# Fewer and larger first loads, two feed-forward tiles by rows of x, and v cast in pairs of heads, in a fused linear-attention and GEGLU kernel

## The chip, the cores and the metric

One core of a Trainium2 chip runs the whole program. The metric is the device time of one execution in microseconds (us), taken over several executions. "Ratio" is the estimate from the fast runs of one kernel and of the kernel before in the same rounds, with a 95% interval; below 1 is faster. "So many us faster" below is the difference of the plain means of all these runs. Only kernels of one set of rounds are compared closely.

## The reference, cut to what matters

```python
# q, k, v: (8 batches, 8 heads, 576 rows, 64), float32
q_s = softmax(q, over the 64 columns of a head)
k_s = softmax(k, over the 576 rows)
kv  = einsum('bhsd,bhse->bhde', k_s, v)           # 64 x 64 per head
x   = einsum('bhsd,bhde->bhse', q_s, kv)          # -> (4608, 512)
out = (gelu(x @ w_gate) * (x @ w_val)) @ w_out    # 512 -> 1536 -> 512
```

## The kernel before

The kernel runs batch by batch on TensorE (PE): feed-forward tiles `psg` and `psv` (12 pairs per batch, eight 128x512 matmuls a pair), then the output product `psy`. The attention of the next batches is threaded between them ("ride"). The parts that the change and the argument touch:

```python
def load(src, nm, b, h0, h1, n0):          # two transfers of 64 partitions each, on SyncE's queue
    ...
    for t in range(2):
        nc.sync.dma_start(out=tiles[key][t:P:2, h0:h1, n0 * D:NC * D], in_=...)

def cast_v(b, h0, h1, eng="pool"):         # f32 -> f16, one instruction
    copy_on(eng, v16_b[b % 2][:, :, h0:h1, 0:D].rearrange("p n h d -> p h n d"),
            tiles[("v", b)][:, h0:h1, :].rearrange("p h (n d) -> p h n d", d=D))

def norm_mul(b, hp, eng="dve"):            # q softmax: e *= 1/sum, both inputs in SBUF
    ...
def warm_pe(n):                            # n matmuls whose result nobody reads
    ...
def ffn_first(xt, after):                  # several tiles at once: rows 0 and 1 of x, then 2, then 3
    ...

# start: twelve first transfers, by halves of the heads
for src, nm, n0 in ((q, "q", 1), (k, "k", 0), (v, "v", 0)):
    for h0 in (0, 4):
        load(src, nm, 0, h0, h0 + 4, n0)
...
# batches 2 to 7: v of all heads cast on GpSimd, one batch ahead
at(b, FI, NFI - 1, L(exp, "q", b + 2), L(exp, "k", b + 2), L(cast_v, b + 2, 0, H))
...
# only batch 1 uses ffn_first
if b == 1:
    hts = ffn_first(xt, first1)
```

Engine names in the profile: DVE is VectorE, ACT is ScalarE, POOL is GpSimd, SP is SyncE.

The softmax here doesn't subtract the row's maximum and nothing guards it: scores larger than these inputs give would overflow.

## Time and profile before

| | before |
|---|---|
| median of the first three runs | 333.1 us (332.79 to 333.62) |
| profiled span | 330.8 us |
| PE busy | 317.1 us, 96% |
| VectorE, ScalarE, GpSimd busy | 56%, 44%, 12% |
| PE's first matmul of the third feed-forward tile of batch 0 | 22.14 us |
| PE's first matmul of batch 1's fourth tile | 59.57 us |
| from there to the end | 271.22 us |

The lines of the profile before stand in the prediction.

### The profile page before, as it was taken

The page shows a single profiled execution, that of the slowest core. Times are in us where ns is not written, and L with a number is a line of the kernel's source. Part 1 is how long each engine was busy: PE and PEld are TensorE (multiplying, and loading weights), DVE is VectorE, ACT ScalarE, POOL GpSimd, SP SyncE. Part 2 cuts the span into 40 slices and gives each one's busy share as a digit, 9 for nine tenths or more (in the row PEclk, how much of TensorE's full clock was granted, in tenths as well). Part 3 has the DMA queues.
Part 4 walks back from the last instruction along what each step waited for, and adds up shares of the span by engine and source line. Part 5 has one row for each costly group of instructions (what it writes and reads, how often), then busy time and mean ns, then how long its engine had stood idle before and what let it go on. Part 6 is the DMA issues. An engine that isn't in the chain of part 4 may idle for free.

```text
span 330.8 us, 4451 instructions
## 1 busy us (share of the span) xinstructions
PE 317.1 (96%) x1700; PEld 151.9 (46%) x1700; DVE 183.9 (56%) x327; ACT 146.7 (44%) x196; POOL 41.0 (12%) x40
## 2 busy tenths in 40 slices
PE   7699999997999999999999999999999999999994
PEld 2334444444455544544454445444544444444441
DVE  4743375499579736962599238832983234333331
ACT  3553564896353582349134932474243033103300
POOL 1377462211000200020002000200000000000000
PEclk9799999999999999999999999999999999999999
DMA  6999999970177015900491029301100110040002
GB/s 189 356 383 391 402 393 391 395 263 0 63 247 294 2 53 164 387 2 0 164 389 53 2 106 355 144 0 65 63 0 2 63 63 2 0 110 17 4 32 95
DMA packets 38453, 50.49 MB, mean 153 GB/s; under 512 B 2208, under 2 KB 34208, under 8 KB 38432
## 3 DMA queue, kind: packets, MB, share of 16 engines
q1 hardware_dynamic: 38288, 50.08, 42.7%
q8 instruction: 13, 0.21, 0.3%
q10 hardware_dynamic: 144, 0.13, 0.1%
q14 instruction: 8, 0.07, 0.1%
HBM read 40.76 MB, written 9.44 MB: 152 GB/s over the span
## 4 chain that ended last, share of the span: by engine, by line
PE 77%; DMA 9%; DVE 5%; ACT 3%; SPq 2%; issue 2%; POOL 1%; DVEq 0%; ACTq 0%; POOLq 0%
PE psy L308 26%; PE psg L264 23%; PE psv L264 22%; DMA wvst<-in_moe_w_val_dram 4%; DMA qt<-in_q_dram 3%; PE pskv L190 2%; DVE eq L163 2%; DMA kt<-in_k_dram 2%; PE psx L242 2%; PE pst L215 2%; DVE rq L156 1%; SPq L103 1%; ACT eq L143 1%; DVE ht L271 1%; ACT L143 1%
## 5 line engine op out<-in xcount | busy, mean ns | idle before, releaser
L269 ACT ACTIVATE gl<-psg 128x512 f32<-128x512 f32 x108 | 64.0, 598 | 140.3 <-PE psg L264 130.3
L271 DVE SCALAR_TENSOR_TENSOR ht<-psv,gl 128x512 f16<-128x512 f32 x108 | 73.8, 688 | 65.3 <-PE psv L264 61.0
L264 PE MATMUL psg<-xt,wg_sb 128*128 128x512 f16 x384 | 100.1, 379 | 0.7 <-ACT xt L121 0.5
L264 PE MATMUL psv<-xt,wv_sb 128*128 128x512 f16 x384 | 99.5, 379 | 0.1
L308 PE MATMUL psy<-wo_sb,ht 128*128 128x512 f16 x432 | 95.8, 379 | 0.0
L264 PEld LDWEIGHTS <-wv_sb 128*128 128x128 f16 x432 | 42.2, 98 | 51.9 <-issue 1.4
L308 PEld LDWEIGHTS <-ht 128*128 128x128 f16 x432 | 41.7, 98 | 48.4 <-DVE ht L271 0.2
L264 PEld LDWEIGHTS <-wg_sb 128*128 128x128 f16 x432 | 40.9, 98 | 45.0 <-issue 1.8
L342 DVE TENSOR_SCALAR yo<-psy 128x512 f32<-128x512 f32 x31 | 21.2, 687 | 48.6 <-PE psy L308 48.6
L119 POOL CAST v<-vt 128x2560 f16<-128x2560 f32 (+1 forms) x7 | 14.9, 2123 | 148.2 <-DMA vt<-in_v_dram 140.6
L156 DVE TENSOR_REDUCE rq<-eq 128x10 f32<-128x640 f16 (+1 forms) x32 | 25.4, 793 | 9.5 <-ACT eq L143 9.3
L163 DVE TENSOR_TENSOR eq<-eq,rrq 128x640 f16<-128x640 f16 (+1 forms) x27 | 26.0, 963 | 0.9
L121 ACT CAST xt<-psx 128x512 f16<-128x512 f32 x27 | 15.1, 587 | 16.8 <-PE psx L242 16.8
L143 ACT ACTIVATE eq<-qt 128x2560 f16<-128x2560 f32 (+1 forms) x9 | 18.5, 2051 | 4.7 <-DMA qt<-in_q_dram 4.6
L143 ACT ACTIVATE ek<-kt 128x2048 f16<-128x2048 f32 (+1 forms) x10 | 15.6, 1560 | 3.7 <-DMA kt<-in_k_dram 3.7
L215 PE MATMUL pst<-ident,eq 128*128 128x128 f16 x128 | 11.1, 226 | 4.9 <-DVE eq L163 2.8
L215 PEld LDWEIGHTS <-eq 128*128 128x128 f16 x128 | 8.7, 100 | 9.9 <-POOL eq L163 2.7
L190 PE MATMUL pskv<-v,ek 128*128 128x130 f16 x160 | 12.0, 220 | 1.2 <-DVE v L123 1.1
L190 PEld LDWEIGHTS <-ek 128*128 128x128 f16 x160 | 10.4, 97 | 4.7 <-issue 1.5
L264 PE MATMUL psg<-xtr,wg_sb 128*128 128x512 f16 x48 | 12.3, 379 | 0.0
L264 PE MATMUL psv<-xtr,wv_sb 128*128 128x512 f16 x48 | 12.3, 379 | 0.0
L242 PE MATMUL psx<-eqt,kv_sb 128*128 128x512 f16 x32 | 10.8, 380 | 1.1 <-DVE kv_sb L198 0.9
(52 smaller groups left out, 131.8 us busy)
## 6 DMA issues: line engine op xcount, KB each, us to landing
qt<-in_q_dram SPq DMA_DIRECT2D x14, 640.0 KB, 6.8
kt<-in_k_dram SPq DMA_DIRECT2D x12, 640.0 KB, 8.2
vt<-in_v_dram SPq DMA_DIRECT2D x12, 640.0 KB, 9.7
out_dram<-yo SPq DMA_DIRECT2D x14, 512.0 KB, 3.1
wost<-in_moe_w_out_dram SPq DMA_DIRECT2D x6, 512.0 KB, 8.8
kt<-in_k_dram SPq DMA_DIRECT2D x8, 320.0 KB, 6.8
vt<-in_v_dram SPq DMA_DIRECT2D x8, 320.0 KB, 6.6
wgst<-in_moe_w_gate_dram SPq DMA_DIRECT2D x5, 512.0 KB, 7.4
```

Of the source, the lines that this page charges most:

```text
L121: nc.scalar.copy(out=dst, in_=src)
L143: nc.scalar.activation(out=dst[:, c0:c1, h0 * D:h1 * D].rearrange("p n (h d) -> p h n d", d=D), in_=tiles[(nm, b)][:, h0:h1, c0 * D:c1 * D ...
L156: nc.vector.reduce_sum(rq, e, axis=mybir.AxisListType.X)
L163: (nc.gpsimd if eng == "pool" else nc.vector).tensor_tensor(out=e, in0=e, in1=rrq.unsqueeze(-1).to_broadcast((P, n, 2, D)), op=ALU.mult)
L190: nc.tensor.matmul(pskv[:, j, :], ek_b[b % 2][:, n, hp * P:(hp + 1) * P], v16_b[b % 2][:, n, 2 * hp:2 * hp + 2, 0:VW], start=(n == 0), sto ...
L215: nc.tensor.transpose(pst[:, j, n * P:(n + 1) * P], eq_b[b % 2][:, n + 1, hp * P:(hp + 1) * P], ident)
L242: nc.tensor.matmul(psx, st[(b, "kv", hp)].rearrange("p h e -> p (h e)"), st[(b, "eqt")][:, hp, 0:MAIN], start=True, stop=True)
L264: nc.tensor.matmul(ps, w[:, ci, fi * P:(fi + 1) * P], xt[:, ci, :], start=(ci == 0), stop=(ci == HP - 1))
L269: nc.scalar.activation(out=gl, in_=psg, func=ACTF.Gelu)
L271: nc.vector.scalar_tensor_tensor(out=ht, in0=psv, scalar=_H_SCALE, in1=gl, op0=ALU.mult, op1=ALU.mult)
L308: nc.tensor.matmul(psy, hts[fi][:, ns * P:(ns + 1) * P], wo_sb[:, fi, :], start=(fi == 0), stop=(fi == NFI - 1))
L342: nc.vector.tensor_scalar(out=yo, in0=psy, scalar1=1.0 / _H_SCALE, scalar2=None, op0=ALU.mult)
```

## The change

Its intent: fewer transfers ahead of the weights, no wait of PE for the last two rows of x before the first feed-forward tile, and no long GpSimd instruction beside VectorE. The order of the start and the warm-up matmuls follow.

```diff
     def cast_v(b, h0, h1, eng="pool"):
+        if eng == "pool" and h1 - h0 > 2:
+            for h in range(h0, h1, 2):
+                cast_v(b, h, h + 2)
+            return
...
     for src, nm, n0 in ((q, "q", 1), (k, "k", 0), (v, "v", 0)):
-        for h0 in (0, 4):
-            load(src, nm, 0, h0, h0 + 4, n0)
+        load(src, nm, 0, 0, H, n0)
...
-    warm_pe(14)
+    warm_pe(16)
...
     unit_t(0, 0, "dve")
-    warm_pe(4)
+    warm_pe(6)
     cast_v(0, 0, 4, "dve")
+    cast_v(0, 4, 6, "act")
     unit_t(0, 1, "dve")
+    cast_v(0, 6, 8, "pool")
     unit_kv(0, 0)
-    warm_pe(2)
-    cast_v(0, 4, 6, "act")
-    cast_v(0, 6, 8, "dve")
+    unit_kv(0, 1)
     unit_x(0, 0, "act", True)
     unit_x(0, 1, "act", True)
-    unit_kv(0, 1)
...
-    unit_x(0, 2, "act", True)
+    unit_x(0, 2, "dve", True)
     unit_x(0, 3, "dve", True)
...
+    first = {0: [[], []], 1: first1}
...
-        if b == 1:
-            hts = ffn_first(xt, first1)
-            fi0 = 3
-            ride(b, FI, 2)
+        if b in first:
+            hts = ffn_first(xt, first[b])
+            fi0 = len(hts)
+            ride(b, FI, fi0 - 1)
```

## The prediction

> **What bounds the kernel now.** I read the page's slices first, then the chain of work that ended last, then the timeline of the places where TensorE (PE) stands idle, and last the transfer rates of the first microseconds.
>
> ```profile
> PE   7699999997999999999999999999999999999994
> PEclk9799999999999999999999999999999999999999
> DMA  6999999970177015900491029301100110040002
> ```
>
> PE is full in nearly all 40 slices of 8.27 us. Of the 330.8 us, the page gives PE 317.1 busy, so at most 13.7 us are to be had in all, and nearly all of it lies in the first two slices and in slice 10. The DMA line is full in slices 1 to 7 only: transfers can bind the first 60 us and nothing later. A change that touches the start and the v casts can therefore move the total by a few microseconds at most.
>
> The chain of waits, in order of time, says what sets the step from batch 0 to batch 1 (columns: start us, us, what):
>
> ```profile
> 29.25 10.23 DMA qt<-in_q_dram
> ...
> 40.84 2.35 ACT eq L143
> ...
> 46.33 1.27 POOL eq L163
> 47.60 0.05 issue
> 47.65 0.40 PE pst L215 x4
> ```
>
> The load of batch 1's q lands at 39.48, and exp, sums and norms follow without slack until PE transposes it at 47.65. In the timeline PE had come to that unit at 47.17 (its first four transposes), so transfer chain and PE arrive there within about 0.26 us of each other. A faster start of PE alone is lost at 47.65, unless the transfer stream is earlier too.
>
> After that PE has only two marked gaps, both in the timeline (start us, us, engine, line, operation):
>
> ```profile
> 73.58 2.32 POOL L119 CAST v<-vt 128x2560 f16<-128x2560 f32 x1 [10.53 <-DMA vt<-in_v_dram]
> 73.60 2.98 DVE L163 TENSOR_TENSOR eq<-eq,rrq 128x640 f16<-128x640 f16 x1
> ...
> 76.64 0.40 PE L215 MATMUL pst<-ident,eq 128*128 128x128 f16 x4 [1.67 <-DVE eq L163]
> ...
> 175.81 2.33 POOL L119 CAST v<-vt 128x2560 f16<-128x2560 f32 x1 [30.99 <-DMA vt<-in_v_dram]
> ...
> 176.15 2.67 DVE L163 TENSOR_TENSOR eq<-eq,rrq 128x640 f16<-128x640 f16 x1
> ...
> 178.87 0.40 PE L215 MATMUL pst<-ident,eq 128*128 128x128 f16 x4 [0.42 <-DVE eq L163]
> ```
>
> The reader should see that the norm multiplication, whose median over the line is 825 ns, took 2.98 and 2.67 us exactly where GpSimd's 2.3 us cast of v began just before it, and ended about 0.7 to 0.8 us after that cast ended; and that PE then waited for it.
>
> The start of batch 0 and its transfers (windows view: stretch, then busy us of PE, PEld, DVE, ACT, POOL, granted clock, DMA share, GB/s):
>
> ```profile
> 15.08 0.73 ACT L121 CAST v<-vt 128x640 f16<-128x640 f32 x1 [1.89 <-DMA vt<-in_v_dram]
> ...
> 15.88 0.88 DVE L123 CAST v<-vt 128x640 f16<-128x640 f32 x1
> ...
> 18.39 1.32 PE L264 MATMUL psg<-xt,wg_sb 128*128 128x512 f16 x4
> ```
> ```profile
> 4.00:6.00 2.00, 2.00 (x6) 0.65 (x5) 0.09 (x1) 1.06 (x1) 0.00 (x0) 1.00 1.01 287
> 6.00:8.00 2.00, 1.34 (x8) 0.49 (x6) 1.93 (x4) 0.11 (x1) 0.00 (x0) 1.00 0.86 230
> ...
> 12.00:14.00 2.00, 0.84 (x7) 0.35 (x4) 0.62 (x2) 1.20 (x2) 0.65 (x1) 0.68 1.07 389
> ```
>
> The second half of v lands at 15.08, and the feed-forward starts at 18.39. The second tile's first matmul is at 20.41; eight matmuls at the 0.216 us spacing seen later give an effective start of 20.41 - 1.73 = 18.68. Transfers run at 230 to 290 GB/s early, against 389 later, although the engines' busy share is near 1.
>
> **What the Trainium skill says.** "SBUF — State Buffer", section "Who interferes with whom", says a VectorE instruction with two SBUF inputs contends with a GpSimd instruction that reads SBUF, and that the loser blocks for the winner's whole instruction. The trace agrees: 2.98 and 2.67 us instead of 0.825. "DMA: Bandwidth & Descriptors", section "Issuing engines are not separate DMA queues", says that parallel issue saves only sequencer time; here the twelve first loads cost 0.62 to 0.89 us of SyncE each, and the first weight load is issued at 9.36, but the queue is never visibly empty, so I expect little from halving the issues. "TensorE: Matmul & The Clock Gate", section "What's actually happening", says that the clock falls after an idle window and needs a busy one to return, in free-running windows; the trace grants 0.50 in 10 to 12 us and full clock from about 13.3.
>
> **Part 1, the casts in pairs.** It removes six 128x2560 casts of 2326 ns median and adds 24 of 128x640. The one cast of that form in the trace took 716 ns, so one batch's v costs 4 x 0.72 = 2.9 us of GpSimd instead of 2.3; GpSimd is 12% busy, and the result is needed a batch later, so this costs nothing. A norm that meets a cast now waits for one piece, at most 0.72 us, if VectorE gets the port between pieces. At 73.60: piece one ends at 74.30, the multiplication at 75.13, and PE transposes at about 75.17 instead of 76.64: 1.47 us. At 176.15: piece one ends at 176.53, the multiplication at 177.36, before PE needs it at 178.28 (four transposes at 0.055 us after 178.06): 178.87 - 178.28 = 0.59 us. The sum is 2.06 us, on the path since PE is saturated from there to the end. A third collision, at 109.44 (1.26 us instead of 0.69), cost PE nothing. I allow a tenth of this for shifted phases and new small collisions: **1.8 us**.
>
> **Part 2, the six loads.** Each carries twice the bytes at, I take it, the same 0.62 to 0.65 us of issue (batch 1's full q loads, deep in the queue, show a minimum of 0.60). SyncE then reaches the weights near 4.7 us instead of 9.36. But the bytes before v is complete are the same: 1.05 MB of q and 1.18 MB each of k and v, 3.41 MB. The early slowness is mostly slow packets (single packets of 0.2 to 1.3 us, against 46 to 55 ns usually, until about 11.5 us), which I see no reason to go away; idle engines are worth some 0.2 of 2 us at 6 to 8, an estimate from the share of 0.86 against 1.07, so about 0.4 us. So v should be complete at 14.7, plus or minus 0.4. The first halves are lost: q, landed by halves at 4.82 and 7.89, now lands whole at 7 to 8, and v's first half no longer comes at 13.40.
>
> From q at 7.5: exp 1.06 to 8.6; VectorE then has four sums (0.68 + 0.20 each) and two multiplications (0.69), 4.9 us, so until 13.5, then the 0.64 us copy, until 14.1. That fits before v. From v at 14.7: VectorE casts half of v (0.83), GpSimd a quarter at the same moment, and these two contend: the 0.88 us of the cast at 15.88, half the size of the 0.83 us one at 13.40, shows that already. So both are done about 1.6 us later, or VectorE's at 0.85 if it wins. Key-value products follow: 20 matmuls, 1.1 us at full clock, 2.2 at half; then 0.8 us for reciprocal and first scaling, 0.4 for the x product, 0.6 for its copy, partly side by side. Effective start: 14.7 + 0.85 + 1.1 + 0.9 + 0.4 = 17.95 in the good case, 18.7 if GpSimd wins, about 19 if the half clock lasts. Against 18.68 that is a gain of 0.7, 0, or a loss of 0.3.
>
> **Part 3, two tiles by rows.** PE does eight matmuls on rows 0 and 1 of x first, 1.73 us of work that covers the two 0.69 us copies of rows 2 and 3, now both on VectorE. This removes the 0.3 us between 18.39 and 18.68 and makes up for the serial copies. It needs the second tile's weights about 0.9 us earlier; their casts end at 17.90 and 18.69 before, needed at about 18.8 and 19.2: just enough.
>
> What the start can pay is limited at 47.65: transfers earlier by 0.4 plus the 0.26 us of slack, and no more than PE's own gain. Good case 0.6, middle 0.2, bad -0.3: **0.3 us**.
>
> Sum: 333.1 - 1.8 - 0.3 = **331.0 us**.
>
> **Rivals.** (A) The large transfers fill the queues earlier and the stream gains 1 to 1.5 us; then PE and the chain at 47.65 both gain it: about 329.8. For it: the low early rate. Against: SyncE is ahead of the data all the time. (B) The start gets slower, since whole-head loads hold up exp and norms, the clock stays low or GpSimd blocks VectorE's v cast: PE comes to 47.65 a microsecond late: 332. For it: q's first half was at work 3 us sooner. (C) VectorE does not get the port between the pieces and waits for all four, 2.9 us instead of 2.3: then part 1 loses some 0.6 us at each of the two gaps, about 334. Against it: the skill's lock is per instruction, and VectorE is already waiting when a piece ends.
>
> **Range and chances.** The middle is 331.0. A and the good case give the low end, 329.5; B with half of part 1 the high end, 332.9. A fall of over 2% needs 326.4 us, about half of all the PE idle time in the span, and no rival reaches it; a rise over 2% needs 339.8, which not even C reaches.
>
> **What would show it.** Right: 24 casts of about 0.72 us from batch 2 on; no multiplication of line 163's norm above about 1.6 us; no PE gap over 0.5 us at batch 2's last transposes near 75 us nor in the middle batches; batch 1's q landing within 0.5 us of 39.5; feed-forward start between 17.8 and 19. Wrong: q of batch 1 landing a microsecond or more away (A), PE reaching batch 1's transposes late (B), or multiplications of 3 us among the pieces (C).

## The result, and the profile after

The changed kernel took 329.15 us median (329.01 to 329.48, 4 runs) against 332.95 us of before (4 runs): ratio 0.9887, interval 0.9866 to 0.9907. That is below the range of the prediction. In two more sets of rounds the same kernel gave 329.61 us (ratio 0.9928) and 329.3 us (ratio 0.9904). The three gains are 3.77, 2.49 and 3.23 us, mean 3.2; the prediction had 2.1.

The page of the changed kernel, its slices (8.2 us each now; tenths of busy time):

```profile
PE   7699999999999999999999999999999999999994
PEclk9599999999999999999999999999999999999999
DMA  7999999960196016900590039202100110040002
```

The 7 in the tenth slice of PE is gone. The granted clock in the second slice is lower than before (5 instead of 7), and yet the time fell.

The timeline of the changed kernel at the place of the large gap, and at the second one (start us, us, engine, line, operation):

```profile
73.18 0.82 DVE L167 TENSOR_TENSOR eq<-eq,rrq 128x640 f16<-128x640 f16 x1
73.22 3.36 POOL L119 CAST v<-vt 128x640 f16<-128x640 f32 x4 [10.70 <-PE psg L268]
...
74.15 0.61 PE L219 MATMUL pst<-ident,eq 128*128 128x128 f16 x8
...
173.18 3.31 POOL L119 CAST v<-vt 128x640 f16<-128x640 f32 x4 [30.23 <-PE psg L268]
...
173.88 1.36 DVE L167 TENSOR_TENSOR eq<-eq,rrq 128x640 f16<-128x640 f16 x1
...
175.79 0.61 PE L219 MATMUL pst<-ident,eq 128*128 128x128 f16 x8
```

The four pieces need 3.3 us where the one cast needed 2.3. At 173.88 the norm waited for the rest of one piece only, 1.36 - 0.82 = 0.54 us, and PE goes through its eight transposes with no gap marked. At 73.18, however, VectorE was simply first, by 0.04 us; one profile cannot say whether the pieces saved anything there. That needed the experiments.

The chain of waits of the changed kernel at the step from batch 0 to batch 1:

```profile
39.33 7.77 PE psy L312 x36
47.10 0.52 PE pst L219 x8
47.61 1.29 PE psy L312 x6
```

Here PE is bound by itself: no transfer, exp or norm stands between 39.33 and 47.61, where before the load of q1 did.

The start of the changed kernel, and its transfers in the windows view (columns as in the prediction):

```profile
14.03 0.83 DVE L123 CAST v<-vt 128x1280 f16<-128x1280 f32 x1 [0.80 <-DMA vt<-in_v_dram]
14.05 1.38 POOL L119 CAST v<-vt 128x640 f16<-128x640 f32 x1 [0.19 <-DMA vt<-in_v_dram]
...
15.17 1.94 PE L194 MATMUL pskv<-v,ek 128*128 128x130 f16 x20
...
18.32 0.72 PE L268 MATMUL psg<-xt,wg_sb 128*128 128x512 f16 x2
```
```profile
4.00:6.00 2.00, 2.00 (x6) 0.65 (x5) 0.00 (x0) 0.00 (x0) 0.00 (x0) 1.00 1.10 372
6.00:8.00 2.00, 1.38 (x6) 0.45 (x4) 0.38 (x1) 1.47 (x2) 0.00 (x0) 1.00 1.01 344
...
12.00:14.00 2.00, 2.00 (x6) 0.72 (x5) 1.20 (x3) 1.54 (x3) 1.04 (x1) 0.50 1.10 369
```

v lands whole at 14.0, the cast of GpSimd lasts 1.38 us since VectorE's came first, and the key-value products run at half clock. The transfers run at 344 to 372 GB/s where they had 230 to 287. The third tile begins at 21.90, against 22.14 before. So this pair of profiles shows a start 0.24 us better at the third tile and 0.42 us at batch 1's fourth tile (59.15 against 59.57), and 268.55 us from there to the end instead of 271.22. That is 0.42 + 2.67 = 3.1 us, the difference of the two spans.

### The profile page after: what moved, and what is told of

It reads as the page before. It is cut to its first block, busy times and chain, and to the rows that moved or that the text cites. A ratio compares the mean times of both kernels' runs of the same rounds, so it can differ in the third digit from the quotient of the medians.

```text
span 327.7 us, 4481 instructions
## 1 busy us (share of the span) xinstructions
PE 317.5 (97%) x1702; PEld 153.1 (47%) x1702; DVE 180.5 (55%) x327; ACT 146.0 (45%) x195; POOL 46.4 (14%) x59
## 4 chain that ended last, share of the span: by engine, by line
PE 89%; DMA 5%; ACT 2%; DVE 2%; issue 1%; SPq 1%; POOL 0%; POOLq 0%; ACTq 0%
PE psy L312 28%; PE psv L268 26%; PE psg L268 26%; DMA kt<-in_k_dram 3%; PE pskv L194 3%; PE pst L219 2%; PE psx L246 2%; DMA qt<-in_q_dram 1%; PE pswarm L260 1%; SPq L103 1%; ACT xt L121 1%; DVE kv_sb L202 0%; PE pstr L231 0%; DVE rq L160 0%; ACT L143 0%
## 5 line engine op out<-in xcount | busy, mean ns | idle before, releaser
L119 POOL CAST v<-vt 128x640 f16<-128x640 f32 x26 | 20.6, 830 | 141.5 <-PE psx L246 64.3
L167 DVE TENSOR_TENSOR eq<-eq,rrq 128x640 f16<-128x640 f16 (+1 forms) x27 | 23.1, 856 | 0.9
L123 DVE COPY eqt<-pst 128x1024 f16<-128x1024 f16 x16 | 10.9, 679 | 0.6 <-PE pst L219 0.6
```

What stands on the lines that cost most here:

```text
L119: nc.gpsimd.tensor_copy(out=dst, in_=src)
L167: (nc.gpsimd if eng == "pool" else nc.vector).tensor_tensor(out=e, in0=e, in1=rrq.unsqueeze(-1).to_broadcast((P, n, 2, D)), op=ALU.mult)
```

## The experiments

Theories. **C**: the whole casts hold VectorE up by chance, differently in each run, and are worth more than the one profile showed. **S**: the extra gain is in the start. **R**: the pieces had no part in it, VectorE won a race by 0.04 us. **I** came after the first set of rounds: the collision of batch 1 is tied to the landing of v, so that in the kernel before it swallows whatever the start gains, and the parts are worth more together than apart.

### The kernel before once more

No edit.

> The kernel before, unchanged, as a control for the runs and a second profile. Theory C (the GpSimd casts of v as one instruction block VectorE's norm by chance, differently from run to run, and are worth more on average than the one profile showed): ratio 1.000, single runs spread over 1 us or more (332.4 to 333.6 so far), and in this second profile the norms that exceed 1.5 us are at other places or of other lengths than at 73.60 and 176.15. Theory S (the extra gain is in the start, the casts are worth the 2.1 us of the first profile): the same two long norms of 2.98 and 2.67 us within 0.2 us, and spread within 0.5 us.

Ratio 0.9995 (0.9976 to 1.0014), runs from 331.67 to 333.12, median 332.53; the profiled span is 330.8 us again. Timeline:

```profile
73.59 2.32 POOL L119 CAST v<-vt 128x2560 f16<-128x2560 f32 x1 [10.49 <-DMA vt<-in_v_dram]
74.22 2.37 DVE L163 TENSOR_TENSOR eq<-eq,rrq 128x640 f16<-128x640 f16 x1
...
76.65 0.40 PE L215 MATMUL pst<-ident,eq 128*128 128x128 f16 x4 [1.07 <-DVE eq L163]
```

The start of this run was worse: the third tile began at 22.93 instead of 22.14. VectorE came to its norm 0.62 us later than in the first profile (74.22 against 73.60). But GpSimd began its cast at the same moment, 73.59 against 73.58, the norm could end only after the cast, and PE's transposes came at 76.65 against 76.64. Between these two profiles the late start was free, so the early one was lost. Theory C was half met: the runs spread by 1.45 us, but the two long norms are at the same places, one of another length.

### Casts in pairs alone

```diff
     def cast_v(b, h0, h1, eng="pool"):
+        if eng == "pool" and h1 - h0 > 2:
+            for h in range(h0, h1, 2):
+                cast_v(b, h, h + 2)
+            return
```

Three sets of rounds, each beside other kernels:

> Before, with the casts in pairs of heads alone. Theory C: 2.6 to 3.3 us faster than before, spread of single runs at most 0.5 us, no norm above 1.6 us, no marked gap of TensorE after 60 us. Theory S: 2.0 us faster or less. Rival R (VectorE won a race by 0.04 us in the profile after, and the pieces had no part in it): under 1 us faster, with some norm still at 2 us or more.

> Casts in pairs alone, again, so that the start's worth with the casts in pairs is read on one chip. Theory I: 1.8 to 2.6 us faster than before, spread over 1 us or more from the start, whose clock windows fall differently in each run. Rival: equal to the changed kernel within 0.3 us.

> Casts in pairs alone, beside the changed kernel. 1.8 to 2.2 us faster than before, as in the two sets before, with a spread of over 1 us of single runs.

Medians 330.44, 330.61 and 330.85 us; ratios 0.9937, 0.9945 and 0.9953; 1.96, 1.90 and 1.53 us faster than before, mean 1.8. The longest norm from batch 2 on was 0.91, 1.35 and 1.11 us, and no gap of PE is marked after 60 us. The first expectation of theory C, 2.6 to 3.3 us, was too high; S had said 2.0 us or less, which fits. The third set fell short of its 1.8 to 2.2 us. R is out: without any of the start's changes no norm reaches 1.5 us.

The spread stayed (329.78 to 331.34 in the first set), and the profiles put it in the start: the third tile began at 23.88, 22.90 and 23.83 us. In the third of these profiles the windows view shows why; the column after POOL is the granted clock:

```profile
14.00:18.00 4.00, 3.47 (x21) 2.31 (x22) 2.16 (x6) 1.64 (x3) 1.93 (x3) 0.50 1.13 355
18.00:20.00 2.00, 1.35 (x8) 0.65 (x6) 0.78 (x3) 0.31 (x2) 1.11 (x3) 0.50 1.02 357
20.00:24.00 4.00, 4.00 (x18) 1.75 (x17) 1.38 (x2) 3.01 (x5) 2.69 (x3) 0.93 1.09 385
```

PE had half its clock until 20.5 us in that run, into the feed-forward.

### The start alone, and the loads alone

The changed kernel with `cast_v` as before (one instruction), and the kernel before with the six loads.

> The changed kernel with v cast in one instruction of all heads again, so loads, rows and order alone. Theory C: 0.4 to 1.0 us faster than before (batch 1's transposes came 0.4 to 0.5 us earlier in the profile after), with single runs spread as widely as before's. Theory S: 1.5 to 1.9 us faster. Rival R: 2 us or more, since then the start moved VectorE ahead of GpSimd.

> Before with six loads of all heads in place of twelve, order and rows as before. If the six loads alone make the transfer stream earlier: 3.41 MB moved by about 12.4 us instead of 13.5, batch 1's q landing near 39.0 instead of 39.5, and time 0 to 0.5 us faster, limited by TensorE's own arrival. If the stream's gain in the profile after was luck of that run: 3.41 MB at 13.2 us or later, and the time up to 0.5 us slower, since the halves are lost and the second half of v is cast on VectorE after the first.

The start alone: 332.68 us, ratio 0.9998 (0.9975 to 1.0021). The loads alone: 332.5 us, ratio 0.9994. Neither moves the time. S is out in its plain form, and C's 0.4 to 1.0 us for the start alone was missed as well. Timeline of the start alone:

```profile
73.55 2.33 POOL L119 CAST v<-vt 128x2560 f16<-128x2560 f32 x1 [10.43 <-DMA vt<-in_v_dram]
74.10 2.45 DVE L163 TENSOR_TENSOR eq<-eq,rrq 128x640 f16<-128x640 f16 x1
...
76.61 0.40 PE L215 MATMUL pst<-ident,eq 128*128 128x128 f16 x4 [1.15 <-DVE eq L163]
```

76.61 against 76.64 and 76.65, after a third tile at 22.33. The cast begins within 0.04 us of the same moment in these three profiles, and PE goes on only when the norm behind it is done. Two things spoil the picture. In this profile PE had already lost 0.49 us at batch 1's transposes, where VectorE's norm at 44.32 took 1.31 us beside a GpSimd cast of w_out. And with the loads alone the cast came earlier:

```profile
72.96 2.32 POOL L119 CAST v<-vt 128x2560 f16<-128x2560 f32 x1 [10.46 <-DMA vt<-in_v_dram]
74.40 1.55 DVE L163 TENSOR_TENSOR eq<-eq,rrq 128x640 f16<-128x640 f16 x1
...
76.01 0.40 PE L215 MATMUL pst<-ident,eq 128*128 128x128 f16 x4 [0.25 <-DVE eq L163]
```

There PE passed this place 0.6 us sooner, and lost it again to a norm of 2.67 us at 106.5. So the moment is not fixed.

The loads do move the transfers. Adding up the packets of the queue, 3.41 MB, as many bytes as the first q, k and v have, were moved by 12.07 to 12.51 us in all seven profiles with six loads, and by 12.98 to 13.60 us in all eleven with twelve: about 1 us sooner. The time does not follow.

### The changed kernel again, and with twelve loads

> The changed kernel as it is, beside the next three on one chip. Theory I (the collision at batch 1's last norm is tied to the landing of v, so in the kernel before it swallows whatever the start gains, and the parts are worth more together than apart): 3.3 to 4.0 us faster than before, single runs within 0.6 us of each other, and 1.0 to 1.8 us faster than the casts alone. Rival (parts simply add: 2.1 for the casts, 0 for the start, and the first rounds were lucky): about 2.1 us faster, like the casts alone.

> The changed kernel a third time, beside the casts in pairs alone, so that the start's worth is read a second time on one chip. Expected from the second set: 2.2 to 3.2 us faster than before and 0.4 to 1.0 us faster than the casts alone. If the first rounds (3.8 us) were the true size: 3.5 us or more. If the start is worth nothing: equal to the casts alone within 0.2 us.

> The changed kernel with the first batch in twelve transfers by halves again. If the six loads give the start its gain (transfer stream a microsecond earlier): at least 0.5 us slower than the changed kernel, 3.41 MB moved only by 13.2 us, batch 1's transposes waiting for the norm. If the order, the rows and the warm-up give it: within 0.2 us of the changed kernel or faster, since q's first half is back at 4.8.

```diff
-        load(src, nm, 0, 0, H, n0)
+        for h0 in (0, 4):
+            load(src, nm, 0, h0, h0 + 4, n0)
```

The changed kernel was 2.49 and 3.23 us faster than before; beside it the casts alone 1.90 and 1.53. So on top of the casts the start is worth 0.59 us in one set and 1.70 us in the other, about 1.1 us, while alone it was worth nothing. Theory I had forecast 3.3 to 4.0 us, 1.0 to 1.8 us over the casts and runs within 0.6 us for the second set, and missed all three (the runs spread by 1.7 us); the third set came out above its forecasts (3.2 and 1.0 us). That the parts do not add is likely but not settled: the interval of the start alone reaches from 0.7 us slower to 0.8 us faster, and the 0.59 us lie in it. The changed kernel with twelve loads took 329.70 us, ratio 0.9926, against 329.61 and 0.9928 on the same chip: the six loads are worth nothing that these runs resolve. Whole heads bring v in one piece at 14.0, while halves bring its first half at 13.1 and its second at 14.8, and the first half's cast and products then lie under the second half's transfer.

### The two tiles by rows, with the casts

The casts in pairs, and `ffn_first` for batch 0; loads, order and warm-up as before.

```diff
+    first = {0: [[], []], 1: first1}
...
-        if b == 1:
+        if b in first:
```

> Casts in pairs and the two first tiles by rows of x, with loads, order and warm-up as before. If the rows pay by themselves: x rows 2 and 3 come about 0.6 to 0.9 us after row 1, which the eight matmuls of rows 0 and 1 cover, so 0.3 to 0.6 us faster than the casts alone. If the start is lost to the clock and to the casts of v: within 0.2 us of the casts alone.

330.36 us, ratio 0.9933, 2.26 us faster than before, and 0.73 us faster than the casts alone in the same rounds (intervals 0.9914 to 0.9953 and 0.993 to 0.9977, so they overlap). The rows seem to pay, a little more than expected; the size is not settled.

### One long instruction, or the total time of GpSimd?

Both do every cast of v from batch 2 on twice in a row: once as a whole in the kernel before, once in pairs.

```diff
-        copy_on(eng, v16_b[b % 2]..., tiles[("v", b)]...)
+        for _ in range(2 if b >= 2 else 1):
+            copy_on(eng, v16_b[b % 2]..., tiles[("v", b)]...)
```

> The kernel before with the cast of v from batch 2 on done twice in a row, each time as one instruction of all heads (the same result). If VectorE waits for one GpSimd instruction at a time, as long as that instruction lasts: norms of 2 to 3 us, now at more places since GpSimd is at it for 4.6 us per batch, none over 3.3 us, and 0.5 to 3 us slower than before. If what counts is GpSimd's total time at the port: single norms of 4 to 5 us and 3 to 6 us slower.

> Before with the casts in pairs, each pair cast twice, so GpSimd is busy 5.7 us per batch in eight pieces, more than twice the time of the kernel before. If the length of one instruction counts: no norm above 1.7 us, no marked gap of TensorE after 60 us, and the time of the casts in pairs done once, about 2.0 us faster than before, within 0.5 us. If the total time at the port counts: slower than before.

Whole: 332.91 us, ratio 1.0013 (0.9983 to 1.0043), not the 0.5 us slower or more that was expected. Pairs: 331.56 us, ratio 0.9969 (0.9941 to 0.9996). Timeline of the whole casts, then of the pairs:

```profile
73.83 5.19 POOL L119 CAST v<-vt 128x2560 f16<-128x2560 f32 x2 [8.17 <-DMA vt<-in_v_dram]
74.43 2.40 DVE L164 TENSOR_TENSOR eq<-eq,rrq 128x640 f16<-128x640 f16 x1
```
```profile
107.42 6.79 POOL L119 CAST v<-vt 128x640 f16<-128x640 f32 x8 [27.11 <-DMA vt<-in_v_dram]
107.50 1.31 DVE L168 TENSOR_TENSOR eq<-eq,rrq 128x640 f16<-128x640 f16 x1
```

With 5.19 us of casts in two instructions the norm waits for the rest of the first and then runs. With 6.79 us in eight it waits for one. What a norm waits for is the length of one instruction, not GpSimd's total time. From batch 1's fourth tile to the end the doubled pairs took 268.42 us, just like all other kernels with pairs, and the doubled whole casts 270.53. The total time of the doubled pairs missed its expectation (0.9 us faster instead of 2.0 within 0.5): in its profile the start was the worst of all, the third tile at 24.50. With four runs and a start that varies this much I take the tail, not the total, as the answer; that the doubling itself costs part of the missing 1.1 us is not excluded.

### Keeping PE busy before the feed-forward

Three kernels have more warm-up matmuls and nothing else changed: the casts alone (26, 12, 3 in place of 14, 4, 2), the changed kernel (34, 8 in place of 16, 6), and the changed kernel with twelve loads (26, 12, 3, 3).

> Casts in pairs, loads and order as before, but 26, 12 and 3 warm-up matmuls in place of 14, 4 and 2, so that TensorE does not stand idle before the first feed-forward. If the clock's fall before the first feed-forward is what the start of the kernel before loses at random (third tile at 22.1, 22.9, 23.9 and 22.9 us in four profiles of that start): no half clock after 7 us, third tile at 21.8 to 22.2, 0.5 to 1.0 us faster than the casts in pairs alone, that is 2.5 to 3.1 us faster than before and equal to the changed kernel, with six loads and rows worth nothing by themselves. If rows and order are what counts: within 0.2 us of the casts in pairs alone, 2.0 faster than before.

> The changed kernel with more warm-up matmuls (34 and 8 in place of 16 and 6), so that TensorE is busy until its first transposes. If the half clock from 9.7 to 16.5 us costs the start: no half-clock window between 7 and 20 us, key-value products at 0.06 us each instead of 0.11, feed-forward start near 17.4 instead of 18.3, and 0.3 to 0.8 us faster than the changed kernel, the rest held by batch 1's q (exp at 39.1 at best follows its landing). If the start is bound by v's transfer and the casts: within 0.2 us of the changed kernel.

> The changed kernel with loads by halves and with warm-up matmuls between all stages of the start (26, 12, 3, 3). A version meant to beat both: no half clock after 7 us, key-value products and x products at full clock, third tile at 21.0 to 21.5 us, and 0.5 to 1.0 us faster than the changed kernel, 3.0 to 3.5 us faster than before. If the start is bound by transfers and casts rather than by the clock: equal to the changed kernel within 0.3 us.

In all three profiles the clock record shows no half clock from 7.2 us at the latest to the last matmul. The casts with warm-up took 330.14 us, ratio 0.9929, 2.27 us faster than before (expected 2.5 to 3.1), with runs from 329.71 to 330.38: a spread of 0.7 us where the casts alone had 1.6 to 1.8. The changed kernel with warm-up took 329.14 us, ratio 0.9907, 0.67 us faster than the changed kernel in the same rounds, as expected, though the intervals overlap; its feed-forward began at 18.07, not near 17.4, and its runs still spread by 1.4 us. At full clock the third tile began at 22.41 with the old start and at 21.65 with the new one, so the clock is not all that divides the two starts. With twelve loads it took 330.02 us, ratio 0.9929, a miss: its third tile came at 21.26, earlier than in any kernel so far, and then

```profile
46.88 2.48 POOL L167 TENSOR_TENSOR eq<-eq,rrq 128x640 f16<-128x640 f16 x2 [1.94 <-DVE rrq L162]
...
48.19 0.40 PE L219 MATMUL pst<-ident,eq 128*128 128x128 f16 x4 [1.10 <-POOL eq L167]
```

PE stood 1.10 us at batch 1's transposes, since the chain behind q1 was late: q1 landed at 40.02, against 39.00 in the profile with six loads and the longer warm-up. This is the cap that the prediction named at 47.65, and it exists. Whether six loads pay here, with a fast start, is not shown: in the other profile of the new order with twelve loads q1 landed at 39.00 too.

### A version meant to beat both

The changed kernel with the longer warm-up, and with batch 1's exp of q in two halves so that its chain starts sooner:

```diff
-    warm_pe(16)
+    warm_pe(34)
...
-    warm_pe(6)
+    warm_pe(8)
...
-    at(0, FI, NFI - 1, L(exp, "q", 1), L(exp, "k", 1, 0, 4),
+    at(0, FI, NFI - 1, L(exp, "q", 1, 0, 4), L(exp, "q", 1, 4, 8), L(exp, "k", 1, 0, 4),
```

> The changed kernel with the longer warm-up (34, 8) and with batch 1's exp of q in two halves, a version meant to beat both. With the long warm-up alone TensorE waited at batch 1's second transposes (47.18) for the chain q landing, exp of all heads 2.34 us, sums, GpSimd's norm. If that chain is what caps the start: halves bring its first norm about 1.0 us sooner, the wait at the transposes goes, and the time is 0.2 to 0.6 us below the long warm-up alone, that is 3.2 to 3.8 us faster than before. If not: like the long warm-up alone, 3.1 us faster.

328.75 us, ratio 0.9891 (0.987 to 0.9911), 3.69 us faster than before and 0.46 us faster than the changed kernel in the same rounds. The wait at the transposes is not there, third tile at 20.99. It beats the kernel before; its advantage over the changed kernel is within the intervals and so not shown.

## Why the prediction was wrong

The profiles side by side, read from the traces. "Whole" and "pairs" are the casts of v; the old start code is identical in its seven profiles. Kernels with other warm-up, or with the rows alone, are left out.

| | profiles | third tile begins | batch 1's fourth tile to the end |
|---|---|---|---|
| old start, whole (before, again, doubled) | 3 | 22.14, 22.93, 23.13 | 271.22, 270.63, 270.53 |
| new start, whole | 1 | 22.33 | 271.58 |
| old start with six loads, whole | 1 | 23.11 | 270.43 |
| old start, pairs (alone three times, doubled) | 4 | 23.88, 22.90, 23.83, 24.50 | 268.40, 268.63, 268.42, 268.42 |
| new start, pairs (the changed kernel) | 3 | 21.90, 21.44, 21.55 | 268.55, 268.55, 268.54 |

Where does PE lose the rest? Matched matmul by matmul with the second profile of the changed kernel, the whole casts fall behind by these times (us):

| whole casts | up to batch 1's fourth tile | at 74 to 77 | at 107 to 110 | at 176 to 180 |
|---|---|---|---|---|
| before | 0.88 | 1.85 | 0 | 0.60 |
| before again | 1.49 | 1.25 | 0 | 0.63 |
| doubled | 1.70 | 1.28 | 0 | 0.47 |
| start alone | 1.38 | 1.32 | 0.88 | 0.36 |
| loads alone | 1.68 | 0.42 | 0.76 | 0.35 |

By the same measure, with pairs no place after batch 1's fourth tile costs more than 0.22 us.

- **Part 1, the casts: right in the mechanism, in the size partly by luck (see the sum below).** Predicted 1.8 us; alone they gave 1.96, 1.90 and 1.53. The norms wait for one piece; the pieces cost GpSimd 2.9 us or more instead of 2.3, and nothing waits for that. Rival C (VectorE waits for all pieces) is ruled out by the norms of all kernels with pairs. Two small readings were off: 2326 ns is the median of seven casts, one of a quarter the size (the six have 2355), and the norms ended 0.68 us after the casts.
- **The step that failed: the start, "0.3 us", by its base "Against 18.68".** I took the start of one profile as the start of the kernel. It is a draw. With the same code the third tile began between 22.14 and 24.50, mean 23.33 over the seven profiles, and the profile I had was the best of the seven. The half-clock windows fall differently in each run, and in bad ones reach into the feed-forward. The new start's four profiles gave 21.44 to 22.33, mean 21.81. So the new start is about 1.5 us better on average by the profiles, where I compared with its luckiest case and found -0.3 to 0.7. By the prediction's own working (the third tile less 16 matmuls, 3.46 us) the new start comes at 18.35 on average, inside its 17.95 to 19; it is the base that was off, 18.68 where the seven profiles average 19.87. In the four profiles of the new start the half clock ended by 16.5 us, before the feed-forward at 18; which of order, rows and warm-up matmuls does how much of that is only partly told apart (rows with the casts 0.73 us, warm-up with the casts about 0.5 by different sets).
- **The limit at 47.65: real, but not binding in the changed kernel.** I allowed the transfers 0.4 us; 3.41 MB came about 1 us earlier, rival A's mechanism, and q1 landed at 38.73, 0.75 us earlier. But the six loads moved no time, so A is not the cause. In the profile after, PE and not the chain of q1 set that moment. With twelve loads and a fast start it did bind, by 1.10 us. Wrong was "transfers can bind the first 60 us and nothing later": v of batch 2 landed at 73.35 in the profile before, and its cast began at 73.58.
- **The sum: what the casts are worth depends on the start, which I had not seen.** Three profiles of the old start with whole casts differ by 0.99 us at the third tile and end within 0.13 us (330.79, 330.82, 330.92): the later PE comes, the less it waits at 74 to 77 us (second table). In the means the start alone is worth nothing, the casts alone 1.8 us, both together about 3.2 us in three sets. In the first pair of profiles it reads otherwise: the start gained 0.42 us, near my 0.3, and the rest of the run 2.67 us against my 1.8, since that early start lost 1.85 us at 74 to 77. So it was partly luck that 1.8 came out for the casts alone. How far this swallowing holds in general is not shown: the 50 runs of the kernel before in the later sets reach from 331.01 to 333.92, no less widely than the 18 of the casts alone (329.67 to 331.96), and two of the five profiles with whole casts lost 0.76 and 0.88 us at a further place.
- **The base.** I subtracted from 333.1, the median of three runs. Later sets of eleven runs have medians of 332.44 to 332.48. The changed kernel's 329.15 in the first rounds was also on the low side (329.61 and 329.3 later). The gain is nearer 3.2 than 3.8, still above my 2.1.
- **Part 3 and the contention of VectorE and GpSimd at the start: as argued.** VectorE won, GpSimd's cast took 1.38 us, and the eight matmuls of rows 0 and 1 cover the two copies on VectorE, 1.29 us.

What stays open: why six larger transfers run faster in the first 10 us. The traces show fewer slow packets (19 to 31 of over 0.2 us begin before 10 us with six loads, 36 to 58 with twelve), but no run tells what makes a packet slow. Open too are what the order, the rows and the warm-up are each worth, and what spreads the runs of the kernel before.

## What to carry to other kernels

When a wait is tied to an outside event such as the landing of a transfer, a gain ahead of it can be swallowed; remove that wait first, and test changes together as well as alone. Where VectorE is seen to wait for a long GpSimd instruction, cut that into short ones, even at a higher total cost (here 3.3 us of GpSimd instead of 2.3). Before building on a microsecond at the start of a kernel, profile the same kernel several times: the clock of PE and the first transfers may differ by more than the change is worth.

## What the Trainium skill lacked or had wrong

- "SBUF — State Buffer", section "Who interferes with whom": the lock per instruction agrees with every profile. What it lacks is the remedy and its size: with back-to-back pieces of 0.72 us VectorE gets in between two of them. The longest norm from batch 2 on was 2.54 us or more in all five kernels with whole casts and 1.36 us at most in all with pairs, even with eight pieces in 6.79 us.
- "TensorE: Matmul & The Clock Gate", section "What's actually happening": it says that the free-running window makes the warm-up vary from run to run and that the penalty is below 1% of a typical span. The runs agree: 22.14 to 24.50 us for the same code, 2.4 us or 0.7% of the span, though not all of it is the clock (v landed between 14.76 and 15.44 us in these seven). It does not say that this is as large as what one compares in a tuned kernel, nor how much work bridges such a start: here some 20 more warm-up matmuls held the full clock through the loads (four of four profiles). The spread of the runs fell from 1.6 to 0.7 us with the casts alone, but stayed at 1.4 us in the changed kernel.
- "DMA: Bandwidth & Descriptors", sections "Issuing engines are not separate DMA queues" and "Rules for kernel authors": the rule to make transfers large points the right way. But no page tells of the slow first 10 us: single packets of 0.2 to 1.3 us among ones of 46 to 55 ns, 230 to 287 GB/s instead of 389, and 3.41 MB moved about 1 us sooner when the first six transfers were large than with twelve small ones, though issue was ahead of the data in both.
